# SwiGLU feed-forward on one Trainium2 core: the order and grouping of the first loads, and of the first matmul groups

## The chip, the cores and the metric

The kernel runs on one core of a Trainium2 chip. The core has a matmul engine (TensorE, PE in the profile, with its weight loads as PEld), VectorE (DVE), ScalarE (ACT), GpSimd (POOL) and SyncE (SP). SP and ACT each have a queue from which they issue DMAs; 16 DMA engines carry them out. The metric is device time in microseconds of one execution; lower is better.

## The reference

```python
B, S, D, F = 1, 2048, 512, 1376        # all bf16

def reference(x, w_gate, w_up, w_down):
    g = silu(x @ w_gate)               # (2048, 512) @ (512, 1376)
    u = x @ w_up
    return (g * u) @ w_down            # (2048, 1376) @ (1376, 512)
```

## The kernel before

F is cut into 10 full tiles of 128 and a rest of 96, the 2048 tokens into four chunks of 512, and D, over which the first products sum, into four blocks of 128. For a chunk and an F tile, four matmuls make the gate (a group "G") in one PSUM bank and four make the up (a group "U") in the next; below, G2 is the gate of F tile 2 and U2 its up. ScalarE applies silu to the gate bank, VectorE multiplies the result with the up bank and stores the hidden tile (`plan_pair`, line 171 and following). The rest of F is packed into groups X and Y. After the four chunks the second product runs over the hidden tiles (lines 396 to 467), and VectorE and ScalarE empty the output banks, which SP stores (lines 253 to 256).

The matmuls need x with D on the partitions. For the first half of chunk 0 (256 tokens) x comes in plainly as two pieces of 128 tokens (`load_xn`, line 112), and PE transposes each with four matmuls against an identity (line 349); VectorE copies the first half of each transposed piece out of PSUM and ScalarE the second half (lines 292 and 281). The other 256 tokens of chunk 0 come by two transposing DMAs (`load_x`, line 92, named x0b and x0c), the other chunks by one each.

The order of work on every engine is written out by hand, and each load has its own semaphore. PE begins with matmuls on constants: `warm(N_WARM, SC)`, five of 512 columns, and `warm(N_FILL, P)`, five of 128 columns (lines 336 to 341). Then it waits for the identity and for each x piece in turn and transposes it. Then come the first eight groups (F tiles 0 to 3 of chunk 0, groups 0 to 7 in eight PSUM banks: G0, U0, G1, U1, G2, U2, G3, U3) in two passes. The first pass takes the first 256 tokens: G0 in two quarters of 128 tokens, so that it can start after one transposed piece, and then groups 1, 2, 3, 4, 6, 5, 7. The second pass takes the other 256 tokens for the same banks, G0 again in two quarters, one for each transposing DMA. From then on a group covers all 512 tokens. A group waits for the load of its weight slab (`need`, line 298, called in `gu_matmuls`, line 315); the slabs of F tiles are listed in `slabs`.

The weight loads (`load_w`, line 97) take a range of columns of w_gate or w_up for all four blocks of D, 128 KB for each F tile. Before, the order of issue is: on SP x piece 0, gate 0, gate 1, up 1, gates 2-3, ups 2-3, the two transposing DMAs, then gates 4-6, ups 4-6, gates 7-10, ups 7-10 and the rest; on ACT x piece 1 and up 0, ahead of a dummy activation that brings in the silu table (line 270).

Of the kernel before, what the change touches and what calls it, by code (L numbers as in the profile page):

```python
# [7 lines left out]
FP32 = mybir.dt.float32  # L8

N_WARM = 5  # L10
N_FILL = 5


def bass_standalone__swiglu_ffn__prompt_kernel(nc, x, w_gate, w_up, w_down, out):
    _, S, D = x.shape
    F = w_gate.shape[1]
    P = 128
    KD = D // P
    NFF = F // P
    NFT = NFF + 1  # L20
# [7 lines left out]
    NXN = HT // P  # L28
# [20 lines left out]
    with ExitStack() as es:  # L49
# [32 lines left out]
        def load_sem(name):  # L82
            loads[name] = sem(f"s_{name}")
            return loads[name]
# [6 lines left out]
        def load_x(eng, name, t0, t1):  # L91
            eng.dma_start_transpose(
                xT_sb[:, :, t0:t1], xf[t0:t1, :]
            ).then_inc(load_sem(name), 16)

        def load_w(eng, name, src, base, f0, f1):
            eng.dma_start(  # L97
                w_sb[:, :, base + f0:base + f1],
                src[:, f0:f1].rearrange("(k p) f -> p k f", p=P),
            ).then_inc(load_sem(name), 16)  # L100

        slabs = [(0, 1), (1, 2), (2, 4), (4, 7), (7, NFT)]
        slab_of = {ft: a for a, b in slabs for ft in range(a, b)}

        def load_gate(eng, a, b):
            load_w(eng, f"wg{a}", w_gate, 0, a * P, min(b * P, F))

        def load_up(eng, a, b):
            load_w(eng, f"wu{a}", w_up, UPH, a * P, min(b * P, F - 32))

        def load_xn(eng, i):
            eng.dma_start(xn_sb[:, i, :], xf[i * P:(i + 1) * P, :]).then_inc(load_sem(f"xn{i}"), 16)  # L112

        def loads_on_scalar(act):
            load_xn(act, 1)
            load_up(act, *slabs[0])

        def loads_on_sync(sp):
            load_xn(sp, 0)
            load_gate(sp, *slabs[0])  # L120
            for a, b in slabs[1:3]:
                load_gate(sp, a, b)
                load_up(sp, a, b)
            load_x(sp, "x0b", HT, HT + P)
            load_x(sp, "x0c", HT + P, SC)
            for a, b in slabs[3:]:
                load_gate(sp, a, b)
                load_up(sp, a, b)
            load_w(sp, "wut", w_up, F - (F - 32), F - 32, F)
            for c in range(1, NSC):  # L130
                load_x(sp, f"x{c}", c * SC, (c + 1) * SC)
            sp.dma_start(
                wd_sb[:, 0:NFF, :], w_down[0:NFF * P, :].rearrange("(k p) d -> p k d", p=P)
            ).then_inc(load_sem("wd"), 16)
            load_sem("wdt")
            for y0 in (0, 64):
                sp.dma_start(wd_sb[y0:y0 + 64, T01, :], w_down[NFF * P:F - SR, :]).then_inc(loads["wdt"], 16)
            for x0 in range(0, P, SR):
                sp.dma_start(wd_sb[x0:x0 + SR, T2, :], w_down[F - SR:F, :]).then_inc(loads["wdt"], 16)
            sp.dma_start(wd_sb[0:F_LAST, TAIL, :], w_down[NFF * P:F, :]).then_inc(load_sem("wdl"), 16)  # L140
# [22 lines left out]
        def tview(i, h):  # L163
            n, b0 = RT[i], T_BANK[i] + RT[i] * h
            return bank_all[:, b0:b0 + n, 0:P // n].bitcast(BF16).rearrange("p b (k t) -> p k b t", k=2)
# [84 lines left out]
        def on_sync(sp):  # L250
            loads_on_sync(sp)
            for t, c0, c1, ob, eng, n in stores:
                sp.wait_ge(s_A if eng == "A" else s_D, n)
                sp.dma_start(of[t * P:(t + 1) * P, c0:c1], o_sb[ob][:, c0:c1]).then_inc(s_out[ob], 16)
            for i in range(NOS):
                sp.wait_ge(s_out[i], 16 * n_store[i])
# [11 lines left out]
        def on_scalar(act):  # L268
            loads_on_scalar(act)
            act.activation(adummy[:, 0:4], zero_c, ACT.Silu)  # L270
            for op in act_ops:
                act.wait_ge(*ready(op))
                if op["kind"] == "silu":
                    if op["free"]:
                        act.wait_ge(s_D, op["free"])
                    fn = ACT.Silu
                else:
                    if op["stored"][1]:
                        act.wait_ge(*op["stored"])
                    fn = ACT.Copy  # L280
                act.activation(op["out"], op["src"], fn).then_inc(s_A, 1)  # L281
# [13 lines left out]
        def on_tensor(pe):  # L295
            landed = set()

            def need(name, count=1):
                if name not in landed:
                    pe.wait_ge(loads[name], 16 * count)  # L300
                    landed.add(name)
# [13 lines left out]
            def gu_matmuls(g, n0, n1):  # L315
                c, ft = g["c"], g["ft"]
                if c > 0:
                    need(f"x{c}")
                if c == 0 and n1 > HT:
                    need("x0b")  # L320
                if c == 0 and n1 > HT + P:
                    need("x0c")
                need(("wg" if g["kind"] == "G" else "wu") + str(slab_of[ft]))
                col = (0 if g["kind"] == "G" else UPH) + ft * P
                for dk in range(KD):
                    if c == 0 and dk % 2 == 0:
                        for i in range(n0 // P, min(n1 // P, NXN)):
                            after(*xt_ready[i, dk // 2])
                    ins = pe.matmul(  # L329
                        g["bank"][:, n0:n1], lhsT=w_sb[:, dk, col:col + P],  # L330
                        rhs=xT_sb[:, dk, c * SC + n0:c * SC + n1], start=(dk == 0), stop=(dk == KD - 1),
                    )
                if n1 == SC:
                    ins.then_inc(s_P, 1)

            def warm(n, width):
                for i in range(n):
                    pe.matmul(banks[NB - 1][:, 0:width], lhsT=ones_w, rhs=ones_m[:, 0:width], start=True, stop=True)  # L338

            warm(N_WARM, SC)  # L340
            warm(N_FILL, P)
            pe.wait_ge(s_I, 1)
            for i in range(NXN):
                need(f"xn{i}")
                for dk in range(KD):
                    for b in range(RT[i]):
                        rt = P // RT[i]
                        r0 = rt * b
                        ins = pe.matmul(  # L349
                            tview(i, dk // 2)[:, dk % 2, b, :], lhsT=xn_sb[r0:r0 + rt, i, dk * P:(dk + 1) * P],  # L350
                            rhs=ident[r0:r0 + rt, r0:r0 + rt], start=True, stop=True, is_transpose=True,
                            tile_position=(r0, 0), skip_group_check=True,
                        )
                        if dk % 2 == 1:
                            ins.then_inc(s_X, 1)

            first = groups[0:NB]
            for n0, n1 in ((0, P), (P, HT)):
                gu_matmuls(first[0], n0, n1)
            for at in (1, 2, 3, 4, 6, 5, 7):  # L360
                gu_matmuls(first[at], 0, HT)
            for n0, n1 in ((HT, HT + P), (HT + P, SC)):
                gu_matmuls(first[0], n0, n1)
# [108 lines left out]
        on_gpsimd(nc.gpsimd)  # L472
        on_scalar(nc.scalar)
        on_tensor(nc.tensor)
        on_vector(nc.vector)

# [27 lines left out]
```

## Time and profile before

| what | value |
|---|---|
| median of 3 runs | 120.71 us (119.93 to 120.72) |
| the profiled execution, its own time | 120.27 us |
| its span in the profile | 119.0 us |
| PE busy in the span | 115.6 us (97%) |
| first matmul on constants | 0.84 us |
| x pieces issued | 0.80 us (ACT) and 0.81 us (SP) |
| first matmul on real weights | 4.48 us |

The profile shows one execution; its times count from the start of the span. PE's busy time is modelled with overlap, so a busy PE is not PE at its peak. The timeline lists instructions in order, merged while the same kind goes on, with the idle time before them in square brackets and what ended it. The chain of waits goes back from the last instruction to whatever released each step. A DMA row gives the queue that issued it (SPq, ACTq), its size, and the time from issue to landing. The table by stretches gives, for each stretch, the busy time and number of instructions of each engine, the granted clock, the DMA engines' share and the GB/s that they moved.

### The profile page before, as it was taken

How to read it: one execution, taken by the hardware profiler on the slowest of the kernel's cores; microseconds unless marked ns; L12 is line 12 of the kernel's file. 1: busy time of each engine (PE TensorE's matmuls, PEld its weight loads, DVE VectorE, ACT ScalarE, POOL GpSimd, SP SyncE). 2: the span in 40 equal slices, each digit the busy share in tenths (PEclk: the TensorE clock that was granted, in tenths of full speed). 3: DMA queues.
4: the chain of work that ended last, by engine and by line, in shares of the span. 5: the costliest groups of instructions: out<-in, count | busy, mean ns of one | idle time of the engine just before them, and what ended most of it. 6: DMA issues, size and time to landing. Idle time of an engine off the chain costs nothing.

```text
span 119.0 us, 2293 instructions
## 1 busy us (share of the span) xinstructions
PE 115.6 (97%) x993; PEld 59.6 (50%) x1001; DVE 37.7 (32%) x57; ACT 34.8 (29%) x60; POOL 1.1 (1%) x7
## 2 busy tenths in 40 slices
PE   7999999999999999999999999999999999999993
PEld 2778444444444444444444444444444445885452
DVE  0105633444434444334444344360000044003320
ACT  4306334362343272442363432430000033003021
POOL 1000000000000000000000000000000000000000
PEclk9999999999999999999999999999999999999999
DMA  2999999992000000000000000000000017200252
GB/s 78 277 190 330 311 165 216 237 357 59 0 6 0 0 0 0 0 0 6 0 0 6 0 0 0 0 0 6 0 6 0 0 59 238 67 0 0 83 187 88
DMA packets 17643, 8.83 MB, mean 74 GB/s; under 512 B 10625, under 2 KB 17633, under 8 KB 17633
## 3 DMA queue, kind: packets, MB, share of 16 engines
q1 hardware_dynamic: 16960, 8.42, 27.5%
q10 hardware_dynamic: 672, 0.26, 0.8%
q8 instruction: 8, 0.13, 0.5%
q14 instruction: 3, 0.02, 0.0%
HBM read 4.75 MB, written 2.10 MB: 58 GB/s over the span
## 4 chain that ended last, share of the span: by engine, by line
PE 92%; DMA 3%; SPq 2%; issue 1%; DVE 0%
PE bank L329 57%; PE bank L426 25%; PE bank L465 7%; DMA w_sb<-in_w_gate_dram 3%; PE bank L377 3%; PE bank L388 2%; SPq L97 1%; SPq L112 0%; DVE o_sb L292 0%
## 5 line engine op out<-in xcount | busy, mean ns | idle before, releaser
L329 PE MATMUL bank<-xT_sb,w_sb 128*128 128x512 bf16 (+2 forms) x355 | 70.0, 355 | 0.4
L329 PEld LDWEIGHTS bank<-xT_sb,w_sb 128*128 128x128 bf16 x360 | 34.2, 98 | 35.3 <-DMA w_sb<-in_w_gate_dram 0.4
L288 DVE TENSOR_TENSOR hT_sb<-sg_sb,bank 128x512 bf16<-128x512 f32 x40 | 27.5, 687 | 40.8 <-PE bank L329 34.5
L281 ACT ACTIVATE sg_sb<-bank 128x512 f32<-128x512 f32 x40 | 23.8, 596 | 41.2 <-PE bank L329 41.2
L426 PE MATMUL bank<-wd_sb,hT_sb 32*128 32x512 bf16 x496 | 29.0, 374 | 0.0
L426 PEld LDWEIGHTS bank<-wd_sb,hT_sb 32*128 32x128 bf16 x496 | 15.3, 93 | 11.5 <-issue 0.4
L292 DVE CAST o_sb<-bank 128x512 bf16<-128x512 f32 (+1 forms) x9 | 5.5, 643 | 31.3 <-PE bank L426 25.9
L281 ACT ACTIVATE o_sb<-bank 128x512 bf16<-128x512 f32 (+1 forms) x8 | 4.3, 582 | 33.6 <-PE bank L426 27.9
L465 PE MATMUL bank<-wd_sb,hT_sb 128*128 128x512 bf16 (+2 forms) x45 | 7.8, 333 | 0.2 <-issue 0.2
L465 PEld LDWEIGHTS bank<-wd_sb,hT_sb 128*128 128x128 bf16 x46 | 4.1, 98 | 4.2 <-issue 0.4
L426 PE MATMUL bank<-wd_sb,hy_sb 32*128 32x512 bf16 (+1 forms) x32 | 5.0, 371 | 0.0
L377 PE MATMUL bank<-xT_sb,w_sb 128*128 128x512 bf16 x14 | 3.8, 379 | 0.1
L288 DVE TENSOR_TENSOR hx_sb<-sgx_sb,bank 32x512 bf16<-32x512 f32 x4 | 2.8, 692 | 3.5 <-ACT sgx_sb L281 3.5
L281 ACT ACTIVATE sgx_sb<-bank 32x512 f32<-32x512 f32 x4 | 2.3, 587 | 4.5 <-PE bank L377 4.5
L338 PE MATMUL bank<-const-bfloat16-1.0 128*128 128x512 bf16 (+1 forms) x10 | 2.8, 466 | 0.8 <-PEq L489 0.8
L426 PE MATMUL bank<-wd_sb,hx_sb 32*128 32x512 bf16 (+1 forms) x16 | 3.0, 371 | 0.0
L377 PEld LDWEIGHTS bank<-xT_sb,w_sb 128*128 128x128 bf16 x16 | 1.6, 98 | 1.9
L281 ACT ACTIVATE sgy_sb<-bank 64x512 f32<-64x512 f32 x4 | 2.4, 590 | 0.1
L338 PEld LDWEIGHTS bank<-const-bfloat16-1.0 128*128 128x128 bf16 x10 | 1.2, 139 | 2.2 <-issue 2.2
L388 PE MATMUL bank<-xT_sb,w_sb 128*64 128x512 bf16 x16 | 1.9, 382 | 0.0
L426 PEld LDWEIGHTS bank<-wd_sb,hy_sb 32*128 32x128 bf16 x32 | 1.6, 93 | 0.6
L292 DVE COPY xT_sb<-bank 128x256 bf16<-128x256 bf16 x2 | 0.6, 292 | 4.1 <-PE bank L349 4.0
(17 smaller groups left out, 8.3 us busy)
## 6 DMA issues: line engine op xcount, KB each, us to landing
out_dram<-o_sb SPq DMA_DIRECT2D x15, 128.0 KB, 1.8
wd_sb<-in_w_down_dram SPq DMA_DIRECT2D x1, 1280.0 KB, 7.4
w_sb<-in_w_gate_dram SPq DMA_DIRECT2D x1, 480.0 KB, 5.4
w_sb<-in_w_up_dram SPq DMA_DIRECT2D x1, 448.0 KB, 6.0
w_sb<-in_w_gate_dram SPq DMA_DIRECT2D x1, 384.0 KB, 3.8
w_sb<-in_w_up_dram SPq DMA_DIRECT2D x1, 384.0 KB, 4.6
w_sb<-in_w_gate_dram SPq DMA_DIRECT2D x2, 128.0 KB, 3.4
w_sb<-in_w_gate_dram SPq DMA_DIRECT2D x1, 256.0 KB, 3.9
```

The source lines that it names most:

```text
L97: eng.dma_start(w_sb[:, :, base + f0:base + f1], src[:, f0:f1].rearrange("(k p) f -> p k f", p=P),).then_inc(load_sem(name), 16)
L281: act.activation(op["out"], op["src"], fn).then_inc(s_A, 1)
L288: ins = dve.tensor_tensor(op["out"], op["a"], op["b"], ALU.mult)
L292: ins = dve.tensor_copy(op["out"], op["src"])
L329: ins = pe.matmul(g["bank"][:, n0:n1], lhsT=w_sb[:, dk, col:col + P], rhs=xT_sb[:, dk, c * SC + n0:c * SC + n1], start=(dk == 0), stop=(dk ...
L338: pe.matmul(banks[NB - 1][:, 0:width], lhsT=ones_w, rhs=ones_m[:, 0:width], start=True, stop=True)
L377: ins = pe.matmul(g["bank"][:, :], lhsT=w_sb[:, dk, XC0:XC0 + P], rhs=xT_sb[:, dk, c * SC:(c + 1) * SC], start=(dk == 0), stop=(dk == KD - 1),
L388: ins = pe.matmul(g["bank"][y0:y1, :], lhsT=w_sb[:, dk, YC0:YC0 + 64], rhs=xT_sb[:, dk, c * SC:(c + 1) * SC], start=(dk == 0), stop=(dk == ...
L426: ins = pe.matmul(g["bank"][:, 0:c1 - c0], lhsT=h, rhs=wd_sb[r0:r0 + SR, w, c0:c1], start=(start and fk == fks[0]), stop=(stop and fk == f ...
L465: ins = pe.matmul(g["bank"][:, 0:c1 - c0], lhsT=h, rhs=w, start=(last and fk == 0), stop=(fk == (NFF if last else NFF - 1)), skip_group_ch ...
```

## The change

The slabs of F tile 1 and of F tiles 2 and 3 become one slab of F tiles 1 to 3, for gates and for ups (384 KB each). SP issues both x pieces one behind the other, then up 0, gates 1-3, ups 1-3, the two transposing DMAs and the rest as before. ACT issues gate 0 alone. On PE the short fills ahead of the first transpose go from five to one, two such matmuls are put between the transposes of piece 0 and those of piece 1, and in the first pass the order of groups 1 to 7 becomes U0, G1, G2, G3, U1, U2, U3.

```diff
-N_FILL = 5
+N_FILL = 1
+N_X = 2
...
-        slabs = [(0, 1), (1, 2), (2, 4), (4, 7), (7, NFT)]
+        slabs = [(0, 1), (1, 4), (4, 7), (7, NFT)]
...
         def loads_on_scalar(act):
-            load_xn(act, 1)
-            load_up(act, *slabs[0])
+            load_gate(act, *slabs[0])
 
         def loads_on_sync(sp):
-            load_xn(sp, 0)
-            load_gate(sp, *slabs[0])
-            for a, b in slabs[1:3]:
-                load_gate(sp, a, b)
-                load_up(sp, a, b)
+            for i in range(NXN):
+                load_xn(sp, i)
+            load_up(sp, *slabs[0])
+            load_gate(sp, *slabs[1])
+            load_up(sp, *slabs[1])
             load_x(sp, "x0b", HT, HT + P)
             load_x(sp, "x0c", HT + P, SC)
-            for a, b in slabs[3:]:
+            for a, b in slabs[2:]:
                 load_gate(sp, a, b)
                 load_up(sp, a, b)
...
             for i in range(NXN):
+                if i > 0:
+                    warm(N_X, P)
                 need(f"xn{i}")
...
-            for at in (1, 2, 3, 4, 6, 5, 7):
+            for at in (1, 2, 4, 6, 3, 5, 7):
                 gu_matmuls(first[at], 0, HT)
```

## The prediction

> **What bounds the kernel now.** I read the page first, then the chain of waits in order of time, then the opening in the timeline, in the DMA issues and in the table by stretches, because the diff touches only the opening.
>
> Parts 1 and 4 of the page: TensorE (PE) is busy 97% of the span, and 92% of the chain that ended last is matmuls.
>
> ```profile
> span 119.0 us, 2293 instructions
> ...
> PE 115.6 (97%) x993; PEld 59.6 (50%) x1001; DVE 37.7 (32%) x57; ACT 34.8 (29%) x60; POOL 1.1 (1%) x7
> ...
> PE 92%; DMA 3%; SPq 2%; issue 1%; DVE 0%
> ```
>
> The chain in order of time: all that is not matmul lies ahead of 6.78 us. SyncE (SP) issues loads one after the other, the fourth weight load (gates of F tiles 2 and 3) lands at 6.74, and from 6.78 PE runs with gaps of 0.05 us.
>
> ```profile
> 0.81 0.39 SPq L112
> ...
> 2.27 0.51 SPq L97
> 2.78 0.04 issue
> 2.82 3.92 DMA w_sb<-in_w_gate_dram
> 6.74 0.05 issue
> 6.78 5.42 PE bank L329 x52
> 12.21 0.05 issue
> ```
>
> So whatever moves the moment from which PE never waits again moves the end by the same amount, and nothing else in this change can. The timeline of PE's weight loads tells what PE waits for in the opening, and that the first matmuls on the second token half (the groups are called G and U with their F tile) start at 8.54:
>
> ```profile
> 4.45 1.43 PEld L329 LDWEIGHTS bank<-xT_sb,w_sb 128*128 128x128 bf16 x16
> 6.04 0.33 PEld L329 LDWEIGHTS bank<-xT_sb,w_sb 128*128 128x128 bf16 x4 [0.17 <-DMA w_sb<-in_w_up_dram]
> 6.78 2.31 PEld L329 LDWEIGHTS bank<-xT_sb,w_sb 128*128 128x128 bf16 x26 [0.41 <-DMA w_sb<-in_w_gate_dram]
> ...
> 8.54 0.15 PEld L329 LDWEIGHTS bank<-xT_sb,w_sb 128*128 128x128 bf16 x2
> ```
>
> From 6.78 to 8.54 PE does 16 matmuls of 256 columns, four groups of four: 1.76 / 16 = 0.110 us each, 0.44 a group. G0's eight quarter matmuls and the waits among them take 4.48 to 5.09 (the next group starts there: 6.04 less the two groups U0 and G1 and 0.07 of waits). Seven groups then need 3.07, so without any wait for a load the second half would start at 8.16. It starts at 8.54: **0.38 us is all that the weight loads cost today**, some 0.3 of it ahead of G2. The profiled execution took 120.27, its span 119.0 and 1.27 around it; the median of the runs, 120.71, lies 0.44 above.
>
> **The change, part by part.** PE's order of first halves becomes U0, G1, G2, G3, U1, U2, U3. SP's issues become x piece 0, x piece 1, up 0, gates 1-3 (384 KB), ups 1-3 (384 KB), two DMA transposes; ScalarE (ACT) issues gate 0 alone. An issue on SP costs 0.45 us apart for an x piece and 0.55 for a weight load (0.81, 1.26 and 2.27, 2.82 in the chain). So SP issues at 0.81, 1.26, 1.71, 2.26, 2.81, and the transposes begin at 3.36 in place of 3.93, and gate 4 some 0.57 us earlier than its 6.82.
>
> *x and G0.* The two pieces landed together (2.7 and 2.9 us after 0.81 and 0.80: 3.49 and 3.69), 256 KB in all. After, piece 0 shares only with gate 0. If the queues take turns by packet, piece 0 (1 KB rows) is in after 160 KB; if they share by bytes, after 256 KB. The stretch below moved 263 to 287 GB/s there, so 96 KB is 0.35: piece 0 lands at 3.3 to 3.7. Piece 1 is in after 320 to 384 KB, 0.25 to 0.5 later than the pair's 3.69: 3.95 to 4.2. I take 3.35 and 3.95, near the ends for turns, since the two pieces, issued 0.01 apart on two queues, landed within 0.2 of each other. G0 ended 1.60 after piece 0 landed, with eight transposes in between; the first four took about 0.43 (fills of the same shape: five are busy 0.7 us, one lasts 0.31, so 0.4 / 4 = 0.1 apart), so it ends 1.17 after piece 1: 5.12, at worst 5.37. Gate 0 is in after 448 to 512 KB, 4.3 to 4.5 (up 0, the last of 512 KB, landed at 4.5 before), about when the first transposed block is ready; a late gate 0 moves 4.48 and not the end of G0 by more than 0.1. The four fills that go (0.43) were hidden: PE still waited for piece 0 at 3.49. Fills now end near 3.04. The two matmuls of N_X (0.21) lie in the wait for piece 1; with that cover gone they cost at most 0.21, which puts G0's end at 5.33, and that in turn is hidden by the next item. ACT issues one DMA less (0.47), so its table load and dummy end earlier; nothing waits there until the copy at 4.25. POOL's queue is untouched.
>
> *Gates 1-3.* U0 runs 5.12 to 5.56 (up 0 is in by 4.5). Then G1 waits for a load three times as large as before. 896 KB must be in. Before, 768 KB were in at 6.00 (ups of tile 1) and 1,024 KB at 6.74: half-way is 6.37. Rows of 768 B replace rows of 256 B for 256 KB of this:
>
> ```profile
> 4.00:4.50 0.50, 0.50 (x7) 0.36 (x6) 0.39 (x2) 0.25 (x1) 0.00 (x0) 1.00 1.18 263
> 9.00:10.00 1.00, 1.00 (x13) 0.90 (x11) 0.11 (x1) 0.60 (x1) 0.00 (x0) 1.00 1.03 329
> ```
>
> (last column GB/s): 256 KB at 263 is 1.0 us, at 329 0.8, so 0.2 is saved: 6.17. From below: 384 KB at 329 (1.2 us) behind up 0's landing at 4.5 is 5.7. From above: the later 384 KB loads took 3.8 and 4.6 us from issue, 2.26 + 4.6 = 6.86:
>
> ```profile
> w_sb<-in_w_gate_dram SPq DMA_DIRECT2D x1, 384.0 KB, 3.8
> w_sb<-in_w_up_dram SPq DMA_DIRECT2D x1, 384.0 KB, 4.6
> ```
>
> I take 6.0, nearer to 6.17 (same stretch, and 2.26 + 3.8 = 6.06) than to 5.7. G1 to G3 then run 6.04 to 7.36.
>
> *Ups 1-3.* 1,280 KB must be in, as for the last load before the transposes today (issue 3.37, 4.2 us, 7.53); less 0.2 is 7.33; bounds 7.0 (5.7 + 1.2) and 2.81 + 4.6 = 7.4. U1 follows G3 without a real wait: 7.37 + 3 x 0.44 = 8.68.
>
> *Second half.* Its transposed blocks landed at 8.23 and 8.63 (issues 3.93 and 5.52, 4.3 and 3.1 us) and are issued 0.57 earlier behind no more bytes. They are needed at 8.68 and 8.90, so they cost nothing; if the blocks did not move at all, they would bind only where the second half starts before 8.4.
>
> *All else:* evictions start after the second halves, loads from F tile 4 on are needed after 12 us, and no other instruction is touched. **Sum:** 8.68 for 8.54, +0.14: 120.27 + 0.14 = 120.4. The wait ahead of G2 has become a wait of about 0.5 ahead of G1. Merging saves issues and bytes ahead of the third gate, and gives it back since the first matmul of three tiles now needs all three.
>
> [...] Early matmuls run at half speed: the by-form rows ahead of the first real matmul against those at its start.
>
> ```profile
> L349 PE MATMUL bank<-ident,xn_sb 128*128 128x128 bf16 x3 | 0.5, 311 | 0.0
> ```
>
> ```profile
> L349 PE MATMUL bank<-ident,xn_sb 128*128 128x128 bf16 x1 | 0.2, 219 | 0.0
> ```
>
> The first row is at 3.92 to 4.00 us, the second at 4.43 to 4.47. So PE came to speed near 4.2, some 3.3 us after its first matmul (0.84). [...]
>
> **Rivals.**
> *A, faster:* gates 1-3 land at 5.7 and ups by 7.0. G1 starts 5.74, U1 7.06, the second half at 8.38: 120.1. With no wait for loads at all it starts at 5.12 + 3.07 = 8.19: 119.9, and with piece 1 in as early as 3.69 at 7.93, where the second transposed block (8.06 at the earliest, needed 0.22 after) just allows it: 119.7. For it: the first two weight loads took 3.0 and 3.3 us to land. Against: the next four took 3.7 to 4.2.
> *B, slower:* the big loads land like the slower rows above, gates at 2.26 + 4.6 = 6.86 and ups as slowly as the next larger gate load (5.4): 8.21. U1 then ends the group at 8.25 + 1.31 = 9.56: 121.3. It decides once gates land after 5.9. Against: those rows had two transposes queued ahead, these have x and up 0.
> [...]
> *Not as said:* if the queues don't favour piece 0, it lands at 3.7 as both do now; G0 ends at 5.4, still hidden by gates 1-3.
>
> **Numbers.** Forecast (within 0.3 of 120.4): 0.55; A 0.27; B 0.10; C 0.08. The likeliest case's own range is 120.1 to 120.7. The runs of before alone reach from 119.93 to 120.72, so the range over the cases is 119.7 to 121.1. It leaves out the far ends of B and C. About 1% is what a measurement of this kernel can tell from no change, 1.2 us here. A cannot give that much by its own sum, B and C barely: faster 0.04, within 1% 0.89, slower 0.07.
>
> **What would show it.** Right: PE's longest idle in the opening ahead of G1, put down to the gate load, 0.4 to 0.6; no wait ahead of U1; the second half at 8.5 to 8.9; transposes issued near 3.4; piece 0 landing earlier and piece 1 later than before. Wrong: gates 1-3 in by 5.6, 311 ns rows after 4.5 (C), a wait over 0.3 ahead of U1 (B), or a wait for the transposed blocks at the second half.

## The result, and the profile after

The changed kernel took 121.55 us (median of 13 runs) against 120.27 (13 runs) before: ratio 1.0095, 95% interval 1.0073 to 1.0116. (The ratio leaves out four runs of the change at 123.1 to 123.5, so it lies under the ratio of the medians.) The forecast was 120.4 with a range to 121.1; it was too low. The profiled execution took 121.34, 1.07 more than the one before.

Page of the changed kernel, parts 1 and 4. PE's busy time hardly grew (116.3 us for 115.6); the share of the chain that is DMA did (4% for 3%).

```profile
PE 116.3 (97%) x999; PEld 59.9 (50%) x999; DVE 37.7 (31%) x57; ACT 35.0 (29%) x60; POOL 1.1 (1%) x7
...
PE 93%; DMA 4%; SPq 1%; DVE 0%; issue 0%
```

Its chain in order of time: the last load that PE waits for is now gates 1-3. Before, it was gates 2-3; gates 1-3 are issued earlier (2.20 for 2.82) and land later (6.93 for 6.74). After it PE never waits, as before.

```profile
2.20 4.73 DMA w_sb<-in_w_gate_dram
6.93 0.05 issue
6.98 16.66 PE bank L329 x108
```

Its weight loads on PE in the timeline (start, length, idle before and what ended it):

```profile
4.07 0.92 PEld L329 LDWEIGHTS bank<-xT_sb,w_sb 128*128 128x128 bf16 x8
5.68 0.44 PEld L329 LDWEIGHTS bank<-xT_sb,w_sb 128*128 128x128 bf16 x4 [0.69 <-DMA w_sb<-in_w_up_dram]
6.97 3.29 PEld L329 LDWEIGHTS bank<-xT_sb,w_sb 128*128 128x128 bf16 x35 [0.85 <-DMA w_sb<-in_w_gate_dram]
...
9.61 0.10 PEld L329 LDWEIGHTS bank<-xT_sb,w_sb 128*128 128x128 bf16 x1
```

G0 ends at 5.05, U0 waits to 5.69 for up 0 (0.64), takes 0.55 in place of 0.44, G1 waits from 6.24 to 6.98 (0.74), then 24 matmuls follow without a wait and the second half starts at 9.61, before at 8.54. That is all of the 1.07: 0.64 + 0.11 + 0.74, less the 0.38 of waits before, less 0.04 by which G0 ends earlier. Of these only the last wait binds: G1 starts when gates 1-3 are in, at 6.98, and without the late up 0 and the slower U0 PE would have waited longer ahead of G1 by as much. So the 1.07 can also be read from the end of the last wait: it moved by 0.20 (6.78 to 6.98), and behind it lie 24 matmuls of the first pass where before lay 16, which is 8 x 0.109 = 0.87 more.

The DMA issues tell the two late loads (size, us from issue to landing): up 0 was issued at 1.74, gates 1-3 at 2.20.

```profile
w_sb<-in_w_up_dram SPq DMA_DIRECT2D x1, 128.0 KB, 3.9
...
w_sb<-in_w_gate_dram SPq DMA_DIRECT2D x1, 384.0 KB, 4.7
```

And the table by stretches (length; busy time of PE, PEld, DVE, ACT, POOL; clock; DMA share; GB/s) tells when the DMA engines moved little. The first line is the kernel before, the other two are the change:

```profile
3.50:4.00 0.50, 0.50 (x6) 0.40 (x5) 0.00 (x0) 0.00 (x0) 0.00 (x0) 1.00 1.28 285
```

```profile
3.50:4.00 0.50, 0.50 (x7) 0.34 (x6) 0.28 (x1) 0.30 (x1) 0.00 (x0) 1.00 0.68 131
4.00:4.50 0.50, 0.50 (x8) 0.50 (x6) 0.29 (x1) 0.17 (x2) 0.00 (x0) 1.00 0.90 159
```

Before, the same stretches moved 285 and 263 GB/s. In the change gate 0's last packet has moved by 3.1 us and that of the x pieces by 3.4 (gate 0 lands at 3.39, the second x piece at 3.73); from then on ScalarE's queue is empty, and only SyncE's queue has work. I call the low rate of this stretch the dip.

### The profile page after: what moved, and what is told of

Read it like the earlier page. It is cut to its first block, busy times and chain, and to the rows that moved or that the text cites. A ratio compares the mean times of both kernels' runs of the same rounds, so it can differ in the third digit from the quotient of the medians.

```text
span 120.1 us, 2295 instructions
## 1 busy us (share of the span) xinstructions
PE 116.3 (97%) x999; PEld 59.9 (50%) x999; DVE 37.7 (31%) x57; ACT 35.0 (29%) x60; POOL 1.1 (1%) x7
## 4 chain that ended last, share of the span: by engine, by line
PE 93%; DMA 4%; SPq 1%; DVE 0%; issue 0%
PE bank L329 57%; PE bank L428 24%; PE bank L467 7%; DMA w_sb<-in_w_gate_dram 4%; PE bank L379 3%; PE bank L390 2%; SPq L113 1%; SPq L98 0%; DVE o_sb L292 0%
## 5 line engine op out<-in xcount | busy, mean ns | idle before, releaser
L329 PEld LDWEIGHTS bank<-xT_sb,w_sb 128*128 128x128 bf16 x360 | 34.8, 99 | 36.1 <-DMA w_sb<-in_w_gate_dram 0.8
L379 PEld LDWEIGHTS bank<-xT_sb,w_sb 128*128 128x128 bf16 x16 | 1.6, 98 | 1.9
```

The source lines that it names most:

```text
L329: ins = pe.matmul(g["bank"][:, n0:n1], lhsT=w_sb[:, dk, col:col + P], rhs=xT_sb[:, dk, c * SC + n0:c * SC + n1], start=(dk == 0), stop=(dk ...
L379: ins = pe.matmul(g["bank"][:, :], lhsT=w_sb[:, dk, XC0:XC0 + P], rhs=xT_sb[:, dk, c * SC:(c + 1) * SC], start=(dk == 0), stop=(dk == KD - 1),
```

## The experiments

All ratios are to the kernel before, run on the same chip. Rates and landings are those of one profiled execution for each kernel; e7, which has the change's loads, shows how far they repeat. Landings are issue plus time to landing. In the traces each load's semaphore gets 16 increments (that each comes from one DMA engine is my guess, and no trace shows it); a landing is the last of them, and where it is split below, the 8th or the 15th is given beside it.

| kernel | 3.5-4.0, 4.0-4.5: GB/s | up 0 in | gates in | ratio (interval) |
|---|---|---|---|---|
| before | 285, 263 | 4.50 | 5.50 (tile 1), 6.74 (2-3) | 1 |
| the change | 131, 159 | 5.64 | 6.93 | 1.0095 (1.0073 to 1.0116) |
| e1 queues only | 57, 201 | 5.10 | 5.56, 7.11 | 1.0029 (1.0005 to 1.0053) |
| e2 slabs and order only | 289, 354 | 4.65 | 6.57 | 1.0033 (1.0011 to 1.0054) |
| e3 fills only | 286, 286 | 4.70 | 5.12, 6.57 | 1.0023 (1.0002 to 1.0044) |
| e4 change, slabs split | 91, 152 | 5.27 | 5.72, 6.46 | 1.0023 (1.0002 to 1.0045) |
| e5 change, up 0 on ACT | 265, 297 | 5.29 | 6.22 | 1.0012 (0.9987 to 1.0037) |
| e6 change, gate 0 and up 0 swapped | 98, 64 | 3.56 | 7.24 | one run, 122.39 us |
| e7 change, fills as before | 94, 118 | 5.79 | 6.99 | 1.0088 (1.0055 to 1.012) |
| e8 before, up 1 on ACT | 269, 238 | 4.60 | 6.04, 7.03 | 1.0014 (0.9992 to 1.0035) |
| e9 change, gates 1-3 on ACT | 301, 317 | 6.03 | 5.82 | 1.0021 (1.0003 to 1.0039) |
| e10 change, spare load on ACT | 383, 278 | 5.48 | 7.42 | one run, 123.55 us |
| e11 change, up 0 on ACT and split | 281, 218 | 4.46 | 5.64, 6.67 | 0.9985 (0.9963 to 1.0006) |
| e12 change, ups 0-3 third on SP | 86, 106 | 7.75 | 8.80 | one run, 124.55 us |

**One part at a time.**

e1:

```diff
         def loads_on_scalar(act):
-            load_xn(act, 1)
-            load_up(act, *slabs[0])
+            load_gate(act, *slabs[0])
...
-            load_xn(sp, 0)
-            load_gate(sp, *slabs[0])
+            for i in range(NXN):
+                load_xn(sp, i)
+            load_up(sp, *slabs[0])
```

> The kernel before with one part of the change: both x pieces on SyncE, gate 0 alone on ScalarE, up 0 third on SyncE; slabs, group order and fills as before. Theory 1 (a load of three F tiles lands late because all of it must land, and its last DMA engine is late): gate 1 is small again, so this costs little: ratio to before 0.998 to 1.003, up 0 in by about 4.6 us. Theory 2 (up 0 in third place, behind both x pieces on one queue, is itself late, and all behind it): up 0 lands near 5.6 as in the changed kernel (5.64), PE waits about 0.6 us for it, and the ratio is 1.004 to 1.008. Theory 3 (the clock: thinner fills): 1.000.

Measured 1.0029. The dip is there (57 GB/s), up 0 is late at 5.10, but PE hardly waits for it: its one long wait in the timeline is for gates 2-3, which now stand sixth on SyncE and not fifth (issued at 3.30 for 2.82). The ratio is in the range of theory 1, the landing of up 0 between the two.

```profile
7.15 2.10 PEld L329 LDWEIGHTS bank<-xT_sb,w_sb 128*128 128x128 bf16 x22 [0.77 <-DMA w_sb<-in_w_gate_dram]
```

e2:

```diff
-        slabs = [(0, 1), (1, 2), (2, 4), (4, 7), (7, NFT)]
+        slabs = [(0, 1), (1, 4), (4, 7), (7, NFT)]
...
-            for at in (1, 2, 3, 4, 6, 5, 7):
+            for at in (1, 2, 4, 6, 3, 5, 7):
```

> The kernel before with the merged slabs of F tiles 1 to 3 and the new order of the first groups; queues and fills as before. Theory 1: gates 1-3 land about 6.9 us, PE waits some 1.2 us ahead of G1, ratio 1.007 to 1.010, nearly the whole loss. Theory 2: gates 1-3 land near 6.2, a wait of 0.7, ratio 1.000 to 1.004. Theory 3: 1.000.

Measured 1.0033. No dip, and the load of three tiles is still waited for: 15 increments were in by 5.68, the last at 6.57. The ratio is in the range of theory 2, the landing between the two.

```profile
6.61 2.63 PEld L329 LDWEIGHTS bank<-xT_sb,w_sb 128*128 128x128 bf16 x25 [0.90 <-DMA w_sb<-in_w_gate_dram]
```

e3:

```diff
-N_FILL = 5
+N_FILL = 1
+N_X = 2
...
             for i in range(NXN):
+                if i > 0:
+                    warm(N_X, P)
```

> The kernel before with one short fill in place of five and two between the transposes; nothing else. Theories 1 and 2: ratio 0.999 to 1.002, no run far above the others. Theory 3: matmuls stay at half speed (0.107 us apart at 128 columns) until about 6 us as in the changed kernel, ratio 1.003 to 1.010, and single runs up to 123 us.

Measured 1.0023, between the theories. Its profiled execution shows no wait for a load at all after 4.8 us and still took 121.19, with matmuls at half speed until near 7 us. Matmuls of 256 columns by form, at 6.2 to 6.8 (420 ns for one) and at 7.5 to 7.9 (272):

```profile
L330 PE MATMUL bank<-xT_sb,w_sb 128*128 128x256 bf16 x5 | 1.3, 420 | 0.0
```

```profile
L330 PE MATMUL bank<-xT_sb,w_sb 128*128 128x256 bf16 x6 | 0.8, 272 | 0.0
```

e4:

```diff
-        slabs = [(0, 1), (1, 4), (4, 7), (7, NFT)]
+        slabs = [(0, 1), (1, 2), (2, 4), (4, 7), (7, NFT)]
...
-            load_gate(sp, *slabs[1])
-            load_up(sp, *slabs[1])
+            for a, b in slabs[1:3]:
+                load_gate(sp, a, b)
+            for a, b in slabs[1:3]:
+                load_up(sp, a, b)
```

> The changed kernel with the slabs split again: gate 1, gates 2-3, up 1, ups 2-3, each a load of its own, issued in the order in which PE uses them; queues, group order and fills as changed. Theory 1: gate 1 lands near 5.6, the wait ahead of G1 goes, ratio to before 1.000 to 1.004. Theory 2: up 0 still lands near 5.6 and PE still waits 0.6 for it, ratio 1.004 to 1.008. Theory 3: as the changed kernel, 1.009.

Measured 1.0023: splitting the slabs alone gives back three quarters of the loss, with the dip as deep as in the change (91, 152 GB/s). PE's waits are small and spread:

```profile
5.31 0.79 PEld L331 LDWEIGHTS bank<-xT_sb,w_sb 128*128 128x128 bf16 x8 [0.21 <-DMA w_sb<-in_w_up_dram]
6.50 1.21 PEld L331 LDWEIGHTS bank<-xT_sb,w_sb 128*128 128x128 bf16 x12 [0.40 <-DMA w_sb<-in_w_gate_dram]
8.06 1.21 PEld L331 LDWEIGHTS bank<-xT_sb,w_sb 128*128 128x128 bf16 x14 [0.36 <-DMA w_sb<-in_w_up_dram]
```

So no part alone makes the whole loss, and theory 1 fits the cure better than the cause. The three parts alone cost 0.29, 0.33 and 0.23%, 0.85 in sum, which their intervals can't tell from the 0.95 of the change.

**Which queue holds what.**

e5:

```diff
         def loads_on_scalar(act):
             load_gate(act, *slabs[0])
+            load_up(act, *slabs[0])
...
-            load_up(sp, *slabs[0])
```

> The changed kernel with up 0 moved back to ScalarE's queue, second behind gate 0; SyncE has one load less ahead of gates 1-3. Issue theory (SyncE's queue alone can't feed the DMA engines: from 3.25 to 4.5 us the changed kernel moved some 60 to 160 KB in half a microsecond, against 130 to 140 before, since the loads issued by then had run out): up 0 lands by 4.4, gates 1-3, issued at 1.74 in place of 2.20, by 6.5, no dip of the rate in that stretch, ratio to before 1.000 to 1.005. Landing theory (the load of three tiles waits for its last engine, whoever issues): gates 1-3 still near 6.9, ratio 1.006 to 1.010.

Measured 1.0012, as the issue theory had it for the ratio: the dip is gone and gates 1-3 land at 6.22. Up 0 did not come by 4.4 (15 increments by 5.20, the last at 5.29); G0 ended near 5.3 in this execution, so PE did not wait for it.

```profile
3.50:4.00 0.50, 0.50 (x6) 0.45 (x5) 0.17 (x1) 0.00 (x0) 0.00 (x0) 1.00 1.11 265
4.00:4.50 0.50, 0.50 (x7) 0.39 (x5) 0.12 (x1) 0.38 (x1) 0.00 (x0) 1.00 1.02 297
```

```profile
6.26 3.01 PEld L329 LDWEIGHTS bank<-xT_sb,w_sb 128*128 128x128 bf16 x31 [0.59 <-DMA w_sb<-in_w_gate_dram]
```

e6:

```diff
         def loads_on_scalar(act):
-            load_gate(act, *slabs[0])
+            load_up(act, *slabs[0])
...
-            load_up(sp, *slabs[0])
+            load_gate(sp, *slabs[0])
```

> The changed kernel with gate 0 and up 0 in each other's place: up 0 alone on ScalarE, gate 0 third on SyncE; PE, which begins with G0, then waits for gate 0. Issue theory: whichever load is third on SyncE is late, so gate 0 lands at 5.1 to 5.7 and up 0 by 3.6. If it were the up matrix itself (its first rows read), up 0 would be the late one. The time is then some 0.5 us over the changed kernel's or less, since gates 1-3 land as late as before this swap.

Gate 0 landed at 5.59 and up 0 at 3.56: the place is late, not the matrix. The time, 1.05 over the profiled execution of the change, was longer than expected, and most of that is the clock: PE idled until 5.64, and then its matmuls ran at half speed (256 columns 0.21 us apart, for 0.109 at full speed) until 8.78, where the record of the granted clock first shows full speed. Gates 1-3 came at 7.24, and PE, still busy with U0, did not wait for them. At full speed G1 would have started with them and the second half at about 9.9 (7.29 + 24 x 0.109, an estimate); it started at 10.66, in the change at 9.61.

e7:

```diff
-N_FILL = 1
-N_X = 2
+N_FILL = 5
+N_X = 0
```

> The changed kernel with five short fills again and none between the transposes. Clock theory (the thinner fills keep matmuls at half speed longer): PE comes to full speed near 4.2 to 5 us in place of 5.9, the ratio falls by 0.001 to 0.003, to 1.006 to 1.009, and runs over 122.5 us go away. If the clock has nothing to do with the fills: ratio 1.0095 as the change, or a little more, since the fills now end after piece 0 has landed.

Measured 1.0088; nothing of the loss that this can resolve comes from the fills. In its profile PE was at half speed until 6.4 (four weight loads from 5.84 took 0.56 us, four from 6.04 in the kernel before 0.33), with five fills, so the fills do not decide it. It is also a second look at the change's loads: up 0 at 5.79, gates 1-3 at 6.99.

e8:

```diff
             load_up(act, *slabs[0])
+            load_up(act, *slabs[1])
...
-            for a, b in slabs[1:3]:
-                load_gate(sp, a, b)
-                load_up(sp, a, b)
+            load_gate(sp, *slabs[1])
+            load_gate(sp, *slabs[2])
+            load_up(sp, *slabs[2])
```

> The kernel before with up 1 issued third on ScalarE in place of fourth on SyncE, so that gates 2-3 are issued at 2.27 and not 2.82; all else as before. Issue theory: gates 2-3 land 0.3 to 0.5 earlier than 6.74, the wait ahead of G2 goes, ratio 0.996 to 0.999. Byte theory (the engines are full and only bytes ahead count): 1.000.

Measured 1.0014: no gain. Gates 2-3, issued 0.55 earlier, landed at 7.03, later than 6.74, because gate 1 (6.04) and up 1 (6.64) came later too. In this execution earlier issue was not earlier landing, so the issue theory in its plain form falls.

**What makes the dip.**

e9:

```diff
             load_gate(act, *slabs[0])
+            load_gate(act, *slabs[1])
...
-            load_gate(sp, *slabs[1])
```

> The changed kernel with gates 1-3 moved to ScalarE's queue, second behind gate 0; up 0 stays third on SyncE, ups 1-3 fourth. One-queue theory (the dip comes when only one queue holds work; with a second one fed, the engines stay busy): no dip from 3.5 to 4.5 us (over 250 GB/s against 131 and 159), up 0 in by 4.9, gates 1-3 by 6.2, ratio to before 1.000 to 1.004. Own-feed theory (whatever stands third on SyncE is fed late, since SyncE's loads are issued later): up 0 still lands at 5.1 to 5.7, while gates 1-3 are early, ratio 1.002 to 1.006.

No dip (301, 317 GB/s), as the one-queue theory has it. But up 0 landed at 6.03, later than either theory said, with 384 KB on the other queue beside it; gates 1-3 were in before it at 5.82. One wait of 0.93 for up 0, none ahead of G1, ratio 1.0021, which both theories allow. A late up 0 beside early gates is what the own-feed theory said, so this run does not decide between them; the table by queue below says more.

e10:

```diff
+        spare = sb("spare", [P, 2, D], BF16)
...
             load_gate(act, *slabs[0])
+            act.dma_start(
+                spare[:, :, :], xf[0:2 * P, :].rearrange("(k p) d -> p k d", p=P)
+            ).then_inc(s_spare, 16)
```

> The changed kernel with a spare load of 256 KB (rows of 1 KB, never read) behind gate 0 on ScalarE. Byte theory: 0.75 us more of bytes ahead, gates 1-3 at 7.6. One-queue theory: the engines stay busy from 3.5 to 4.5, up 0 lands at 5.0 or earlier in spite of more bytes, gates 1-3 no later than 6.9. Own-feed theory: up 0 and gates 1-3 land as before this edit, 5.6 and 6.9, as the spare bytes only fill idle time.

Between all three: no dip from 3.5 to 4.0 (383 GB/s), up 0 a little earlier (5.48), gates 1-3 0.49 later (7.42), of the 0.75 that the bytes would cost.

e11:

```diff
-        slabs = [(0, 1), (1, 4), (4, 7), (7, NFT)]
+        slabs = [(0, 1), (1, 2), (2, 4), (4, 7), (7, NFT)]
...
             load_gate(act, *slabs[0])
+            load_up(act, *slabs[0])
...
-            load_up(sp, *slabs[0])
-            load_gate(sp, *slabs[1])
-            load_up(sp, *slabs[1])
+            for a, b in slabs[1:3]:
+                load_gate(sp, a, b)
+            for a, b in slabs[1:3]:
+                load_up(sp, a, b)
```

> The changed kernel with both cures: up 0 second on ScalarE, and gate 1, gates 2-3, up 1, ups 2-3 as loads of their own in the order of use. If the two costs only mattered together (late feed times large slab), this is no better than either cure alone: 1.000 to 1.003. If they add up, it is the best of all and may beat the kernel before: 0.997 to 1.000.

Measured 0.9985 (0.9963 to 1.0006): the lowest ratio of all, clearly under the change, and not shown to be faster than the kernel before. It lies where adding costs put it, but its interval overlaps that of e5, so whether the costs add up is not settled.

e12:

```diff
-            load_up(sp, *slabs[0])
-            load_gate(sp, *slabs[1])
-            load_up(sp, *slabs[1])
+            load_w(sp, "wu0", w_up, UPH, 0, 4 * P)
+            load_gate(sp, *slabs[1])
```

> The changed kernel with ups 0-3 as one load of 512 KB (rows of 1 KB) third on SyncE in place of up 0 and ups 1-3; U0 then waits for all of it, so the time itself is longer by about 0.5 us or more. Only the rate tells: if the dip comes from many short rows, 3.5 to 4.5 us shows over 250 GB/s; if it comes from the third place on a lone queue, whatever the rows, it dips as in the changed kernel, to 130 to 160 GB/s.

It dips as deep with rows of 1 KB:

```profile
3.50:4.00 0.50, 0.50 (x7) 0.37 (x5) 0.29 (x1) 0.10 (x1) 0.00 (x0) 1.00 0.63 86
4.00:4.50 0.50, 0.50 (x7) 0.50 (x7) 0.12 (x1) 0.28 (x1) 0.00 (x0) 1.00 0.94 106
```

Short rows are not the cause. All six kernels with one load on ScalarE's queue (the change, e1, e4, e6, e7, e12) moved 57 to 131 GB/s from 3.5 to 4.0; all eight with two or more moved 265 to 383. The transposing DMAs are not the cause either: e1 dips, and issues its first at 4.61.

The DMA view of the same half microsecond, by queue (q1 is SyncE's, q10 ScalarE's; packets, MB, share of the 16 engines' time), for the kernel before, the change and e9:

```profile
q10 hardware_dynamic: 425, 0.11, 94.8%
q1 hardware_dynamic: 154, 0.04, 32.9%
```

```profile
q1 hardware_dynamic: 252, 0.07, 68.2%
```

```profile
q10 hardware_dynamic: 189, 0.15, 96.1%
q1 hardware_dynamic: 10, 0.01, 3.4%
```

SyncE's queue moved little there in every kernel: 5 to 64 KB in all fourteen traces, and the 64 are the change's. Where ScalarE's queue held a second load, it moved the rest (0.11 MB before, 0.15 in e9), and SyncE's moved no more beside it (0.04 and 0.01 MB, 0.07 in the change). **That the engines move less there with loads on SyncE's queue alone is shown (57 to 131 GB/s for 265 to 383); why is open.** In the dip single packets of 256 B to 1 KB took up to 0.5 us in the change and up to 1.2 in e6; in the first 10 us of the change the median is 18 ns for 256 B, 36 for 768 B and 46 for 1 KB. But packets of 0.4 to 0.6 us stand outside the dip too (before, 0.42 us after 4.5), and the engines were also idle (their share was 0.36 in e1), so long packets are not all of it. What the rest is was not tested.

## Why the prediction was wrong, point by point

- *What bounds the kernel* was right in the sum and wrong in one sentence. The start of the second half moved by 1.07 us (8.54 to 9.61), and the time by 1.07. The moment from which PE never waits again moved by 0.20 alone (6.78 to 6.98), so it does not move the end "by the same amount": two groups more lie behind it now. The sum went by the second half and has this right.
- *x and G0*: right in direction and better than said. Piece 0 landed at 2.94 (said 3.35), piece 1 at 3.73 (3.95), gate 0 at 3.39 (4.3 to 4.5), G0 ended at 5.05 (5.12). That the end of G0 fits is luck in part: it came 1.32 after piece 1 and not 1.17, with the transposes and G0 at half speed (their matmuls of 128 columns start 0.107 us apart, G0's before 0.056).
- **"up 0 is in by 4.5" failed first.** It took the landing of up 0 from a kernel where it stood on ScalarE's queue. In third place on SyncE it landed at 5.64, in the dip, and U0 waited 0.64. By itself this cost nothing in the profiled execution: U0 ended at 6.24, and G1 could not start before 6.98.
- **"I take 6.0" for gates 1-3 is the step that made the miss**, and its upper bound failed too, 6.86 against 6.93. From G1 on PE runs 24 matmuls of the first pass without a wait: 6.04 to 8.68 in the forecast, 6.98 to 9.61 measured. The 0.93 by which the load came late is the whole miss (+1.07 for +0.14). The bytes were right: by 6.0 us the engines had moved 1,034 KB, before 1,047. What failed is reading a landing off the bytes. The 16 increments of one load drift apart: for gates 1-3 the 8th came at 5.88, the 15th at 6.19, the last at 6.93. With up 0 on ScalarE (e5) it was 5.50, 5.81, 6.22. The dip is not needed for it: in e2, without one, it was 5.46, 5.68, 6.57. A load of three tiles waits for the last increment of all three; split (e4), tile 1 comes at 5.72 and PE has work.
- Late queue and large slab are not independent in the change: taking back either one gives 1.0012 (e5) or 1.0023 (e4) for 1.0095, 0.83 and 0.72%, together more than the loss. That they cost more together than apart is not shown (each alone 1.003, e1 and e2). With intervals of 0.2% the sizes of the parts below that are not settled.
- *Ups 1-3 and the second half* cost nothing, as said, but by luck. Ups landed at 8.00 (said 7.33, at most 7.4), and PE needed them at 8.30 only because gates 1-3 were late; had G1 started at 6.04, U1 would have waited from 7.37 to 8.00. The transposed blocks landed at 8.60 and 9.26, later than before (8.23 and 8.63) though issued earlier, and were needed at 9.61 and 9.83. So with these landings right gates alone would not have saved the forecast: the second half would have started at about 9.4 (8.05 + 1.31, an estimate), for 8.68.
- *Rival A* fell. *Rival B* came nearest and had 0.10: gates at 6.86 (6.93), the second half at 9.56 (9.61), 121.3 (121.34). Its ups at 8.21 came at 8.00, and the wait over 0.3 ahead of U1 that was to be its sign did not come; nor does its own sum hold one (6.90 + 1.32 = 8.22, for 8.25). Why the loads land like the slower rows it did not say. *"Not as said"* fell: piece 0 was favoured.
- *C*, given 0.08, had its sign, 311 ns rows after 4.5, and not its loss: PE came to speed between 5.7 and 6.0, for 4.2 before (in the change matmuls of 256 columns start 0.189, 0.147 and then 0.109 us apart from 5.69 on). This slowed G0, and U0 by 0.11, all of it hidden by the wait for gates 1-3. That thinner fills hold back full speed, which its chance rests on, no run shows: half speed lasted until near 7 with them alone (e3), but until 6.4 with five fills (e7). At full speed the second form takes 273 ns (before, from 5.1 on). The changed kernel by form, at 4.95 to 5.2, and at 5.68 to 5.8:

```profile
L329 PE MATMUL bank<-xT_sb,w_sb 128*128 128x128 bf16 x3 | 0.5, 306 | 0.0
```

```profile
L329 PE MATMUL bank<-xT_sb,w_sb 128*128 128x256 bf16 x1 | 0.4, 390 | 0.4 <-DMA w_sb<-in_w_up_dram 0.4
```

- The chances: within 1% was given 0.89, and the ratio 1.0095 is just inside. The range was too narrow: it left out B's own 121.3, though B's landing stood on a row of a load of the same size (4.6 us from issue, here 4.73).

With up 0 on ScalarE's queue more changes than the time of issue: e5 issues gates 1-3 0.47 us earlier than the change, they land 0.71 us earlier, and it takes about 1.0 us less (1.0095 less 1.0012, of 120.3), with the rate from 3.5 to 4.0 at 265 in place of 131 GB/s. It is not so for every such move: e8, which also moves one load to ScalarE, where no dip was (285 GB/s before), gained nothing (1.0014).

## What to carry to other kernels

Price a load at the start of a kernel by when its last part lands, not by the bytes ahead of it (by 6.0 us 1,034 KB had moved here for 1,047 before, and gates 1-3 were in at 6.93), and look at the rate in each half microsecond: where it fell to half of what it was before (131 for 285 GB/s), the next landings slipped here (up 0 from 4.50 to 5.64). Keep two queues filled until the first burst is over (e5: 1.0012 for 1.0095), though where nothing dips one more load on the second queue may gain nothing (e8: 1.0014). Do not merge the loads that the first matmuls wait for: the merged load freed no matmul until all of it was there, at 6.93; split (e4), tile 1 was in at 5.72. Ask how much work lies behind the last wait, and not only when it ends: here it ended 0.20 us later and cost 1.07. Test such edits apart and together: each part alone cost a third of a per cent or less.

## What the runs showed of the hardware that was not expected

In e10 and e12 a stretch of 3.41 us in which PE idled 44 and 73% of the time was followed by one at half speed. In e10 PE idled 1.6 us for gates 1-3; then the granted clock (the number ahead of DMA share and GB/s) halved for one stretch and came back:

```profile
4.40:7.70 3.30, 1.81 (x19) 1.05 (x18) 0.29 (x1) 0.45 (x2) 0.00 (x0) 1.00 1.38 290
7.80:11.10 3.30, 3.30 (x18) 2.37 (x16) 0.00 (x0) 0.00 (x0) 0.00 (x0) 0.50 0.98 276
11.30:14.60 3.30, 3.30 (x36) 3.01 (x35) 1.31 (x2) 1.64 (x3) 0.00 (x0) 1.00 1.16 337
```

The record of the granted clock changes at 4.37, 7.78 and 11.19 us, 3.41 apart. In e12, with 2.65 us idle, it changes at 4.71, 8.12 and 11.54, again 3.41 apart. At half speed for 3.4 us PE loses 1.7 us of work (half of 3.41, an estimate), as much as the wait itself in e10: with gates 1-3 0.49 us later than in the change this makes 2.2, and e10's profiled execution took 2.2 more (123.55 for 121.34). In the 3.41 us from the first change PE idled 1.49 us in e10 and 2.49 in e12; in e9 it idled 0.76 (4.37 to 7.78), and the clock stayed. What lies between was not tried, and idle time was not varied by itself, so the cause is argued from these traces and not shown.
